# Dynamic convolution and max-out MLP on one core: columns taken in rotated order, and the last weight rows in single loads

## The chip, the cores and the metric

The kernel runs on one core of one Trainium2 chip. Its engines work side by side, each on its own queue of instructions: PE (TensorE, matrix products; PEld are its weight loads), DVE (VectorE, elementwise work), ACT (ScalarE, activations and copies), POOL (GpSimd, here mostly an issuer of DMAs) and SP (SyncE, an issuer of DMAs). 16 DMA engines move data between HBM and the on-chip memory SBUF, whose 128 partitions are the rows of every tile. The metric is the device time of one execution in microseconds (us); a time given for a kernel is the median of several runs.

## The reference

There are 8 sequences of 4160 tokens, 192 features each, and for each token 8 heads with 7 generated weights. Each head mixes a token with the six before it, and the result goes through a max-out MLP:

```python
w = softmax(weight_gen)                       # (8, 4160, 8 heads, 7 taps)
x_pad = concat([zeros(8, 6, 192), x], axis=1) # six zero tokens ahead of every sequence
y[b, s, h, :] = sum(w[b, s, h, k] * x_pad[b, s + k, h, :] for k in range(7))
g = maximum(y @ w1, y @ w2)                   # w1, w2: 192 x 1024
out = g @ w_out                               # 1024 x 192
```

The kernel computes the max-out as relu(y (w2 - w1)) @ w_out + y (w1 @ w_out).

## The kernel before, in words

**Tiling.** The 33280 tokens are laid out with 260 consecutive ones in each of 128 partitions; token number c of each partition is called column c. 16 partitions (RPB) hold one sequence. A token needs the six before it (PAD), so column 0 of a partition needs the last six columns of the partition before, and zeros in every 16th partition, where a sequence starts. These six columns are the halo.

**Batches, pieces, units.** Columns are taken in 17 batches (BATCHES, line 50): 16 of 16 columns, then one of 4. A batch is multiplied and added up in pieces (line 53): of 4 columns in the first two batches, of 8 later, and one of 4 in the last batch. Each piece is one unit: its result y_t is turned around into yt, by PE (sum_transpose) in the first two batches, by a DMA transpose on SP (transpose, line 212) later. A unit of 8 columns gives 8 tiles of hidden products; a unit of 4 gives 4, whose products are 256 wide instead of 512, and twice as many (chunks, line 270).

**A column's way.** load_wg (line 101) brings the generated weights, load_x (line 110) the columns of x as bf16, load_halo (line 123) the six columns ahead of a batch, copied out of the batch before in SBUF. ACT takes exponentials (exp_sum), DVE sums them (red), ACT takes the logarithm (ln), DVE subtracts it (shift), ACT takes exponentials again (weights: en_t). DVE multiplies x by the weights for all seven taps in one instruction (mul, line 173, into m_t) and adds the taps in three (adds, line 188). After the turn, PE makes hidden tiles (hid_tile, line 291, from wd = w2 - w1), ACT takes Relu (relu, line 306, into rd_t), PE makes the outputs (out_first, out_second) from rd_t with wo = w_out and from yt with w10 = w1 @ w_out, ACT copies them out of PSUM (evac, line 377) and SP stores them.

**Order.** The order is written out by hand (a manual schedule). Hidden tiles go in groups (GROUPS), two at a time at the start and three later, and each group has a list of output columns made beside it (OUTS). The steps of the convolution are tied to tile numbers: extra (line 758) says at which tile of batch b the multiplications, additions and transposes of batch b + 1 are issued, and the table due (line 731) when the exponentials are. transpose(u) also issues stores that were held back, and lets POOL wait for the transposed tile (gate) before it issues the next loads of x.

**The start** (lines 520 to 630). SP loads, in this order: the generated weights of batch 0; the halo of batch 0 into xs, in two loads of 15 and 112 partitions, partition 0 being zeroed by DVE; columns 0 to 3; the first halves (512 of 1024 columns) of rows 0 to 127 of w1 and w2 (ws0E, ws1E); the last 64 rows of both (ws0T, ws1T), each in two loads, columns 0 to 511 into partitions 0 to 63 and columns 512 to 1023 into partitions 64 to 127; columns 4 to 7; the second halves of ws0E and ws1E; the generated weights of batch 1. POOL and DVE build a mask msk that is 0 in every 16th partition; DVE and ACT multiply the halo by it (lines 568 and 570) into xb_t. On DVE follow the cast of columns 0 to 3 (line 574), the first multiplication, the differences of the weights' first halves (line 584) and of the last 64 rows (line 589), the cast of columns 4 to 7 (line 620) and the second multiplication. ACT and DVE then copy parts of the differences across the partition halves (lines 586, 587 and 591). PE is kept busy by products that nobody reads (keep_warm, line 612) until the first tiles are there.

**The end.** The last transposes stand in the order of extra; evac stores the last units in smaller parts, and the very last pair of column groups goes out from o_last through ACT's and SP's queues.

Of the kernel before, what the change touches and what calls it, by code (L numbers as in the profile page):

```python
# [23 lines left out]
def kernel(  # L24
# [9 lines left out]
    nc = tc.nc  # L34
# [15 lines left out]
    BATCHES = [(c, min(16, CPP - c)) for c in range(0, CPP, 16)]  # L50
    NB = len(BATCHES)


    def pieces(b):
        n = BATCHES[b][1]
        at, done = [], 0
        for w in (4, 4, 4, 4) if b < 2 else (8, 8) if n == 16 else (n,):
            at.append((done, w))
            done += w
        return at  # L60
# [40 lines left out]
    def load_wg(b, eng):  # L101
        c0, n = BATCHES[b]
        wg_ts[b] = pwg.tile([P, n * WGC], FP32, name="wg_t", tag="wg")
        return eng.dma_start(
            out=wg_ts[b],
            in_=bass.AP(tensor=weight_gen.tensor, offset=c0 * WGC,
                        ap=[[CPP * WGC, P], [1, n * WGC]]),
        )

    def load_x(b, o, n, halo=True):  # L110

        if b not in xb_ts:
            xb_ts[b] = pxb.tile([P, (16 + PAD) * D], BF16, name="xb_t", tag="xb")
        load = nc.gpsimd.dma_start(  # L114
            out=xb_ts[b][:, (PAD + o) * D:(PAD + o + n) * D],
            in_=bass.AP(tensor=x.tensor, offset=(BATCHES[b][0] + o) * D,
                        ap=[[CPP * D, P], [1, n * D]]),
        )
        if b > 0 and o == 0 and halo:
            load_halo(b)  # L120
        return load

    def load_halo(b):

        if b not in xb_ts:
            xb_ts[b] = pxb.tile([P, (16 + PAD) * D], BF16, name="xb_t", tag="xb")
        nc.gpsimd.dma_start(out=xb_ts[b][:, 0:PAD * D],
                            in_=xb_ts[b - 1][:, 16 * D:(16 + PAD) * D])
# [183 lines left out]
    def column(c):  # L312

        b = min(c // 16, NB - 1)
        for u, (ub, o, n) in enumerate(UNITS):
            if ub == b and o <= c - BATCHES[b][0] < o + n:
                k = c - BATCHES[b][0] - o
                return u, k // 2, k % 2
# [58 lines left out]
    def evac(p, n):  # L377
# [3 lines left out]
        if p == NT // 2 - 1:  # L381

            nc.scalar.copy(out=_sub(o_last, 0, [[D, 2], [1, D]]),
                           in_=_sub(tile_, at, [[512, 2], [1, D]]))
            for j, eng in enumerate((nc.scalar, nc.sync)):
                eng.dma_start(
                    out=bass.AP(tensor=out.tensor, offset=(place(p)[0] + 2 * j) * D, ap=[[CPP * D, P], [1, D]]),
                    in_=o_last[:, j * D:(j + 1) * D],
                )
            return  # L390
# [7 lines left out]
        for q in range(p, p + n):  # L398
            u, i, _ = column(2 * q)
            if u == NU - 2 and i % 2:  # L400
# [5 lines left out]
        for eng, c, *ap in stores:  # L406

            def issue(eng=eng, c=c, ap=ap, o=o):
                eng.dma_start(
                    out=bass.AP(tensor=out.tensor, offset=c * D, ap=[[CPP * D, P], *ap]),  # L410
                    in_=_sub(o, c % 24 * D, ap),
                )
# [96 lines left out]
    msk_i = consts.tile([P, 1], I32, name="msk_i")  # L509
    msk = consts.tile([P, 1], FP32, name="msk")  # L510
# [3 lines left out]
    with tc.tile_pool(name="pstage", bufs=1) as pstage:  # L514
# [6 lines left out]
        nc.vector.memset(xs[0:1, 0:PAD * D], 0.0)  # L521
        for p0, p1 in ((1, 16), (16, P)):
            nc.sync.dma_start(
                out=xs[p0:p1, 0:PAD * D],
                in_=bass.AP(tensor=x.tensor, offset=(p0 * CPP - PAD) * D,
                            ap=[[CPP * D, p1 - p0], [1, PAD * D]]),
            )
# [3 lines left out]
        def load_first(o):  # L531
            nc.sync.dma_start(
                out=xs[:, (PAD + o) * D:(PAD + o + 4) * D],
                in_=bass.AP(tensor=x.tensor, offset=o * D, ap=[[CPP * D, P], [1, 4 * D]]),
# [12 lines left out]
        for wi, wsrc in enumerate((moe_w1, moe_w2)):  # L547
            for h in range(2):
                nc.sync.dma_start(
                    out=ws["T", wi][half(h), :],  # L550
                    in_=bass.AP(tensor=wsrc.tensor, offset=P * F + h * HF, ap=[[F, 64], [1, HF]]),
                )
# [4 lines left out]
        nc.gpsimd.iota(msk_i, pattern=[[0, 1]], base=0, channel_multiplier=1)  # L557
        make_identity(nc, ident_f)
        nc.vector.tensor_single_scalar(out=msk_i, in_=msk_i, scalar=RPB - 1, op=ALU.bitwise_and)
        nc.vector.tensor_single_scalar(out=msk_i, in_=msk_i, scalar=1, op=ALU.min)  # L560
        nc.vector.tensor_copy(out=msk, in_=msk_i)
        nc.vector.tensor_copy(out=ident, in_=ident_f)  # L562
        for step in (exp_sum, red, ln, shift):
            for i in range(2):
# [3 lines left out]
        nc.vector.tensor_scalar(out=xb_ts[0][:, 0:HP], in0=xs[:, 0:HP], scalar1=msk[:, 0:1], scalar2=None,  # L568
                                op0=ALU.mult)
        nc.scalar.activation(out=xb_ts[0][:, HP:PAD * D], in_=xs[:, HP:PAD * D], func=AF.Copy,  # L570
                             scale=msk[:, 0:1])
# [160 lines left out]
    for c in range(3, NB):  # L732
        soon = c < 8
        parts_ = [(AT.get(('W', c, 0), 16 * (c - 2) + (8 if soon else 10 if c < NB - 1 else 15)), True, lambda c=c: weights(c, 0))]
        if 8 in dict(pieces(c)):
            parts_.append((AT.get(('W', c, 8), 16 * (c - 2) + (14 if soon else 15)), True, lambda c=c: weights(c, 8)))
        if c > 3:
# [20 lines left out]
    def extra(t):  # L758
# [14 lines left out]
        if s == 8 + later and b + 2 < NB:  # L773
            adds(b + 1, 8, beside=lambda i, of: red(b + 3, i, 2) if b + 3 < NB and i < 2 else None)
        if k == n // 4 - 1 and 7 < u + 1 < NU:
# [56 lines left out]
```

## Time and profile before

| what | value |
|---|---|
| median of 3 runs | 409.88 us (408.94 to 411.68) |
| profiled execution: span, first to last instruction | 408.8 us |
| its time outside the span | not on the page; the median above is 1.1 us over the span |
| PE busy | 399.1 us (98%) |
| DVE busy | 373.4 us (91%) |
| ACT busy | 357.2 us (87%) |
| POOL busy | 75.5 us (18%) |
| granted PE clock, mean | 0.999 |
| moved by DMA | 65.68 MB, mean 161 GB/s |

Times in the profile are us from the first instruction. Busy time is not yet a bound: PE's busy time includes the products that keep it warm. The page gives, for groups of instructions, the busy time, the mean of one and the idle time ahead of them with what ended it; the chain that ended last follows the last instruction back to what released it. DVE's last instruction ends at 379.3 us, PE's last at 405.0; the two last stores are issued at 405.5.

### The profile page before, as it was taken

How to read it: one execution, taken by the hardware profiler on the slowest of the kernel's cores; microseconds unless marked ns; L12 is line 12 of the kernel's file. 1: busy time of each engine (PE TensorE's matmuls, PEld its weight loads, DVE VectorE, ACT ScalarE, POOL GpSimd, SP SyncE). 2: the span in 40 equal slices, each digit the busy share in tenths (PEclk: the TensorE clock that was granted, in tenths of full speed). 3: DMA queues.
4: the chain of work that ended last, by engine and by line, in shares of the span. 5: the costliest groups of instructions: out<-in, count | busy, mean ns of one | idle time of the engine just before them, and what ended most of it. 6: DMA issues, size and time to landing. Idle time of an engine off the chain costs nothing.

```text
span 408.8 us, 16064 instructions
## 1 busy us (share of the span) xinstructions
PE 399.1 (98%) x7386; PEld 317.5 (78%) x7386; DVE 373.4 (91%) x217; ACT 357.2 (87%) x424; POOL 75.5 (18%) x101
## 2 busy tenths in 40 slices
PE   7899999999999999999999999999999999999996
PEld 2688999777777877778777777877787776787796
DVE  5999999999999999999999999999999999999100
ACT  6799999999899998999998999998999888988872
POOL 0311011222221022221111222220121221210000
PEclk9999999999999999999999999999999999999999
DMA  8958477667647854965785397478649638643704
GB/s 240 229 118 217 126 148 164 159 150 182 148 102 198 226 129 98 260 167 85 214 231 117 91 256 186 74 243 168 146 98 250 169 59 223 177 88 108 187 35 161
DMA packets 60784, 65.68 MB, mean 161 GB/s; under 512 B 47631, under 2 KB 49039, under 8 KB 60718
## 3 DMA queue, kind: packets, MB, share of 16 engines
q1 hardware_dynamic: 52334, 40.54, 35.6%
q0 software_dynamic: 8240, 24.04, 29.5%
q8 instruction: 57, 0.93, 0.9%
q10 hardware_dynamic: 144, 0.10, 0.1%
q14 instruction: 9, 0.07, 0.1%
HBM read 35.96 MB, written 25.56 MB: 150 GB/s over the span
## 4 chain that ended last, share of the span: by engine, by line
PE 78%; DVE 7%; ACT 7%; DMA 5%; issue 1%; SPq 1%; DVEq 0%; ACTq 0%
PE op_ps L339 36%; PE hd L299 33%; PE op_ps L351 7%; ACT rd_t L309 4%; DVE m_t L182 4%; DMA ws1T<-in_moe_w_dram 2%; DMA out_dram<-o_t 1%; PE hdp L299 1%; PE yps L248 1%; DVE m_t L204 1%; DVE m_t L198 1%; DMA yt<-y_t 1%; ACT en_t L167 1%; ACT o_t L395 1%; DVE y_t L207 0%
## 5 line engine op out<-in xcount | busy, mean ns | idle before, releaser
L309 ACT ACTIVATE rd_t<-hd 128x1024 bf16<-128x1024 f32 (+1 forms) x206 | 234.4, 1188 | 27.8 <-PE hd L299 26.6
L339 PE MATMUL op_ps<-wo,rd_t 64*128 64x192 bf16 x4160 | 211.4, 243 | 0.4 <-issue 0.3
L339 PEld LDWEIGHTS <-rd_t 64*128 64x128 bf16 x4160 | 181.5, 94 | 16.2 <-issue 0.5
L299 PE MATMUL hd<-yt,wd 64*128 64x512 bf16 (+1 forms) x1584 | 187.8, 360 | 0.9 <-DMA yt<-y_t 0.7
L182 DVE TENSOR_TENSOR m_t<-xb_t,en_t 128x10752 bf16<-128x10752 bf16 (+1 forms) x37 | 187.4, 5070 | 0.2
L299 PEld LDWEIGHTS <-wd 64*128 64x128 bf16 x1776 | 94.8, 94 | 42.4 <-issue 2.0
L224 POOL CAST gate<-yt 128x1 f32<-128x1 bf16 x29 | 41.0, 1415 | 264.6 <-DMA yt<-y_t 264.6
L198 DVE TENSOR_TENSOR m_t<-m_t 128x4608 bf16<-128x4608 bf16 (+1 forms) x31 | 75.5, 2434 | 0.1
L395 ACT COPY o_t<-op_ps 128x384 f32<-128x384 f32 (+1 forms) x99 | 57.1, 588 | 13.4 <-PE op_ps L339 13.4
L351 PE MATMUL op_ps<-w,yt 64*128 64x192 bf16 x780 | 55.9, 243 | 0.2 <-ACT o_t L395 0.2
L351 PEld LDWEIGHTS <-yt 64*128 64x128 bf16 x780 | 38.5, 94 | 16.5 <-issue 1.3
L204 DVE TENSOR_TENSOR m_t<-m_t 128x3072 bf16<-128x3072 bf16 (+1 forms) x29 | 50.0, 1723 | 0.1
L167 ACT ACTIVATE en_t<-wg_t 128x896 bf16<-128x896 f32 (+2 forms) x45 | 35.6, 817 | 0.0
L207 DVE TENSOR_TENSOR y_t<-m_t 128x1536 bf16<-128x1536 bf16 (+1 forms) x29 | 27.3, 941 | 0.5
L114 POOL DMA_DIRECT2D xb_t<-in_x_dram x33 | 17.6, 534 | 29.9 <-ACT rd_t L309 18.9
L156 DVE TENSOR_TENSOR wg_t<-wg_t,sum_t 128x280 f32<-128x280 f32 (+5 forms) x46 | 22.0, 480 | 0.0
L147 DVE TENSOR_REDUCE sum_t<-e_t 128x64 f32<-128x448 f32 (+2 forms) x31 | 19.6, 635 | 2.6 <-ACT e_t L135 2.5
L135 ACT ACTIVATE e_t<-wg_t 128x896 f32<-128x896 f32 (+2 forms) x18 | 16.1, 901 | 2.5 <-DMA wg_t<-in_weight_gen_dram 2.5
L309 ACT ACTIVATE rd_t<-hdp 128x1024 bf16<-128x1024 f32 x16 | 16.2, 1031 | 0.6 <-PE hdp L299 0.4
L615 PE MATMUL warm<-ident 128*128 128x512 bf16 x38 | 11.5, 474 | 2.6 <-DVE ident L562 2.6
L299 PE MATMUL hdp<-yt,wd 64*128 64x256 bf16 x192 | 13.5, 270 | 0.3 <-issue 0.2
L248 PE MATMUL yps<-ident,m_t 64*128 64x64 bf16 x600 | 10.5, 191 | 1.5 <-DVE m_t L182 1.5
(45 smaller groups left out, 65.0 us busy)
## 6 DMA issues: line engine op xcount, KB each, us to landing
out_dram<-o_t SPq DMA_DIRECT2D x27, 768.0 KB, 4.9
xb_t<-in_x_dram POOLq DMA_DIRECT2D x30, 384.0 KB, 5.1
wg_t<-in_weight_gen_dram POOLq DMA_DIRECT2D x14, 448.0 KB, 5.4
xb_t<-xb_t POOLq DMA_DIRECT2D x16, 288.0 KB, 5.2
out_dram<-o_t SPq DMA_DIRECT2D x10, 384.0 KB, 3.3
wg_t<-in_weight_gen_dram SPq DMA_DIRECT2D x2, 448.0 KB, 4.5
xs<-in_x_dram SPq DMA_DIRECT2D x2, 384.0 KB, 6.7
xb_t<-in_x_dram POOLq DMA_DIRECT2D x3, 192.0 KB, 5.0
```

What stands on the lines that cost most here:

```text
L156: nc.vector.tensor_tensor(out=w_t, in0=w_t, in1=_sub(s_ts[b], hs.start, [[1, hs.stop - hs.start], [0, K]]), op=ALU.subtract)
L167: nc.scalar.activation(out=_sub(en_ts[b], (o * WGC + j * N * K) * 2, [[2 * N, K], [2, N], [1, 2]]), in_=_sub(wg_ts[b], (o * H + j * N) * K ...
L182: return nc.vector.tensor_tensor(out=m_out, in0=x_in, in1=_sub(en_ts[b], o * WGC * 2, [[2, K * n * H], [0, G // 2], [1, 2]]), op=ALU.mult,)
L198: nc.vector.tensor_tensor(out=taps(0, 1, 3), in0=taps(0, 1, 3), in1=taps(3, 1, 3), op=ALU.add)
L204: nc.vector.tensor_tensor(out=taps(0, 2, 2), in0=taps(0, 2, 2), in1=taps(1, 5, 2), op=ALU.add)
L207: nc.vector.tensor_tensor(out=_sub(y_ts[b], o * D, [[64, 2], [P, 3 * w // 2], [1, 64]]), in0=taps(0, 1, 1), in1=taps(2, 1, 1), op=ALU.add,)
L224: nc.gpsimd.tensor_copy(out=gate, in_=yt[:, 0:1])
L299: nc.tensor.matmul(hid_out(t, f, j), lhsT=wd_at(j, s, f // 4, f % 4 * P, P), rhs=_sub(yt_ts[u][half(j), :], (s + j) % 3 * P, [[3 * P, w // ...
L309: relu_of[t0] = nc.scalar.activation(out=rd[:, k * 1024:(k + n) * 1024], in_=hd[:, at:at + n * 1024], func=AF.Relu)
L339: return nc.tensor.matmul(op_out(c), lhsT=rd[half(r), k * 1024 + at:k * 1024 + at + P], rhs=wo[half(r), f * D:(f + 1) * D], start=False, s ...
L351: nc.tensor.matmul(op_out(c + j), lhsT=yt_ts[u][half(j), (3 * i + (s + j) % 3) * P:(3 * i + (s + j) % 3 + 1) * P], rhs=w10[half(j), s * D: ...
L395: nc.scalar.copy(out=_sub(o, c % 24 * D, [[D, len(qs)], [h * D, 2], [1, D]]), in_=_sub(tile_, at + (qs[0] - p) * D, [[D, len(qs)], [512, 2 ...
```

## The change

Columns are taken in the order 8 to 259, then 0 to 7. The batches stay 17: 15 of 16 columns, one of 12 and one of 8. dcol turns a place in this order into a column in memory, in every load and store.

The halo of the first batch is then columns 2 to 7 of the partition itself, for all 128 partitions: one load, no zeroed partition, no mask, and the two masking products become copies. The halo of the last batch (columns 0 to 7) is what the first one was: the last six columns of the partition before, loaded by POOL from memory into partitions 1 to 127, then zeros into every 16th partition by a second DMA, from a tile of zeros that POOL fills at the start.

The last batches are multiplied in pieces of 8, 4 (batch 15) and 4, 4 (batch 16), with the issue points that these need. Of the stores, the one in two parts stays with a last-but-one unit of 8 columns, which there is no more.

The last 64 rows of w1 and w2 come in one load each: into all 128 partitions, with the source walked as 2 column halves, 64 rows, 512 columns.

```diff
--- before.py
+++ after.py
@@ -47,14 +47,19 @@
     assert RPB * CPP == S
 
 
-    BATCHES = [(c, min(16, CPP - c)) for c in range(0, CPP, 16)]
+    ROT = 8
+    BATCHES = [(c, min(16, CPP - ROT - c)) for c in range(0, CPP - ROT, 16)] + [(CPP - ROT, ROT)]
     NB = len(BATCHES)
+
+    def dcol(c):
+
+        return (c + ROT) % CPP
 
 
     def pieces(b):
         n = BATCHES[b][1]
         at, done = [], 0
-        for w in (4, 4, 4, 4) if b < 2 else (8, 8) if n == 16 else (n,):
+        for w in (4, 4, 4, 4) if b < 2 else (8, 8) if n == 16 else (8, 4) if n == 12 else (4, 4):
             at.append((done, w))
             done += w
         return at
@@ -103,7 +108,7 @@
         wg_ts[b] = pwg.tile([P, n * WGC], FP32, name="wg_t", tag="wg")
         return eng.dma_start(
             out=wg_ts[b],
-            in_=bass.AP(tensor=weight_gen.tensor, offset=c0 * WGC,
+            in_=bass.AP(tensor=weight_gen.tensor, offset=dcol(c0) * WGC,
                         ap=[[CPP * WGC, P], [1, n * WGC]]),
         )
 
@@ -113,7 +118,7 @@
             xb_ts[b] = pxb.tile([P, (16 + PAD) * D], BF16, name="xb_t", tag="xb")
         load = nc.gpsimd.dma_start(
             out=xb_ts[b][:, (PAD + o) * D:(PAD + o + n) * D],
-            in_=bass.AP(tensor=x.tensor, offset=(BATCHES[b][0] + o) * D,
+            in_=bass.AP(tensor=x.tensor, offset=dcol(BATCHES[b][0] + o) * D,
                         ap=[[CPP * D, P], [1, n * D]]),
         )
         if b > 0 and o == 0 and halo:
@@ -124,8 +129,15 @@
 
         if b not in xb_ts:
             xb_ts[b] = pxb.tile([P, (16 + PAD) * D], BF16, name="xb_t", tag="xb")
-        nc.gpsimd.dma_start(out=xb_ts[b][:, 0:PAD * D],
-                            in_=xb_ts[b - 1][:, 16 * D:(16 + PAD) * D])
+        if b < NB - 1:
+            nc.gpsimd.dma_start(out=xb_ts[b][:, 0:PAD * D],
+                                in_=xb_ts[b - 1][:, 16 * D:(16 + PAD) * D])
+            return
+        nc.gpsimd.dma_start(
+            out=xb_ts[b][1:P, 0:PAD * D],
+            in_=bass.AP(tensor=x.tensor, offset=(CPP - PAD) * D, ap=[[CPP * D, P - 1], [1, PAD * D]]),
+        )
+        nc.gpsimd.dma_start(out=xb_ts[b][0:P:RPB, 0:PAD * D], in_=zeros[0:P:RPB, :])
 
 
     def exp_sum(b, i=0, of=1):
@@ -311,10 +323,9 @@
 
     def column(c):
 
-        b = min(c // 16, NB - 1)
-        for u, (ub, o, n) in enumerate(UNITS):
-            if ub == b and o <= c - BATCHES[b][0] < o + n:
-                k = c - BATCHES[b][0] - o
+        for u, (b, o, n) in enumerate(UNITS):
+            k = c - BATCHES[b][0] - o
+            if 0 <= k < n:
                 return u, k // 2, k % 2
 
     def place(p):
@@ -384,7 +395,7 @@
                            in_=_sub(tile_, at, [[512, 2], [1, D]]))
             for j, eng in enumerate((nc.scalar, nc.sync)):
                 eng.dma_start(
-                    out=bass.AP(tensor=out.tensor, offset=(place(p)[0] + 2 * j) * D, ap=[[CPP * D, P], [1, D]]),
+                    out=bass.AP(tensor=out.tensor, offset=dcol(place(p)[0] + 2 * j) * D, ap=[[CPP * D, P], [1, D]]),
                     in_=o_last[:, j * D:(j + 1) * D],
                 )
             return
@@ -397,7 +408,7 @@
         stores = []
         for q in range(p, p + n):
             u, i, _ = column(2 * q)
-            if u == NU - 2 and i % 2:
+            if u == NU - 2 and UNITS[u][2] == 8 and i % 2:
                 stores.append((nc.sync, place(q)[0] - 1, [4 * D, 2], [1, 2 * D]))
             elif u < NU - 1 and i == UNITS[u][2] // 2 - 1:
                 stores.append((nc.sync, place(q)[0] - i, [1, 2 * (i + 1) * D]))
@@ -407,7 +418,7 @@
 
             def issue(eng=eng, c=c, ap=ap, o=o):
                 eng.dma_start(
-                    out=bass.AP(tensor=out.tensor, offset=c * D, ap=[[CPP * D, P], *ap]),
+                    out=bass.AP(tensor=out.tensor, offset=dcol(c) * D, ap=[[CPP * D, P], *ap]),
                     in_=_sub(o, c % 24 * D, ap),
                 )
 
@@ -506,8 +517,7 @@
     wo = consts.tile([P, FCH * D], BF16, name="wo")
     w10 = consts.tile([P, 3 * D], BF16, name="w10")
     ident = consts.tile([P, P], BF16, name="ident")
-    msk_i = consts.tile([P, 1], I32, name="msk_i")
-    msk = consts.tile([P, 1], FP32, name="msk")
+    zeros = consts.tile([P, PAD * D], BF16, name="zeros")
     gate = consts.tile([P, 1], FP32, name="gate")
     o_last = consts.tile([P, 2 * D], FP32, name="o_last")
 
@@ -518,20 +528,17 @@
               for kind, w in (("E", F), ("T", HF)) for wi in range(2)}
 
         load_wg(0, nc.sync)
-        nc.vector.memset(xs[0:1, 0:PAD * D], 0.0)
-        for p0, p1 in ((1, 16), (16, P)):
-            nc.sync.dma_start(
-                out=xs[p0:p1, 0:PAD * D],
-                in_=bass.AP(tensor=x.tensor, offset=(p0 * CPP - PAD) * D,
-                            ap=[[CPP * D, p1 - p0], [1, PAD * D]]),
-            )
+        nc.sync.dma_start(
+            out=xs[:, 0:PAD * D],
+            in_=bass.AP(tensor=x.tensor, offset=(ROT - PAD) * D, ap=[[CPP * D, P], [1, PAD * D]]),
+        )
 
         nc.scalar.preload_act_table_set("natural_log_exp_and_others")
 
         def load_first(o):
             nc.sync.dma_start(
                 out=xs[:, (PAD + o) * D:(PAD + o + 4) * D],
-                in_=bass.AP(tensor=x.tensor, offset=o * D, ap=[[CPP * D, P], [1, 4 * D]]),
+                in_=bass.AP(tensor=x.tensor, offset=dcol(o) * D, ap=[[CPP * D, P], [1, 4 * D]]),
             )
 
         load_first(0)
@@ -545,30 +552,24 @@
 
         load_w(0)
         for wi, wsrc in enumerate((moe_w1, moe_w2)):
-            for h in range(2):
-                nc.sync.dma_start(
-                    out=ws["T", wi][half(h), :],
-                    in_=bass.AP(tensor=wsrc.tensor, offset=P * F + h * HF, ap=[[F, 64], [1, HF]]),
-                )
+            nc.sync.dma_start(
+                out=ws["T", wi],
+                in_=bass.AP(tensor=wsrc.tensor, offset=P * F, ap=[[HF, 2], [F, 64], [1, HF]]),
+            )
         load_first(4)
         load_w(1)
         load_wg(1, nc.sync)
 
-        nc.gpsimd.iota(msk_i, pattern=[[0, 1]], base=0, channel_multiplier=1)
+        nc.gpsimd.memset(zeros, 0.0)
         make_identity(nc, ident_f)
-        nc.vector.tensor_single_scalar(out=msk_i, in_=msk_i, scalar=RPB - 1, op=ALU.bitwise_and)
-        nc.vector.tensor_single_scalar(out=msk_i, in_=msk_i, scalar=1, op=ALU.min)
-        nc.vector.tensor_copy(out=msk, in_=msk_i)
         nc.vector.tensor_copy(out=ident, in_=ident_f)
         for step in (exp_sum, red, ln, shift):
             for i in range(2):
                 step(0, i, 2)
         xb_ts[0] = pxb.tile([P, (16 + PAD) * D], BF16, name="xb_t", tag="xb")
         HP = PAD * D // 4
-        nc.vector.tensor_scalar(out=xb_ts[0][:, 0:HP], in0=xs[:, 0:HP], scalar1=msk[:, 0:1], scalar2=None,
-                                op0=ALU.mult)
-        nc.scalar.activation(out=xb_ts[0][:, HP:PAD * D], in_=xs[:, HP:PAD * D], func=AF.Copy,
-                             scale=msk[:, 0:1])
+        nc.vector.tensor_copy(out=xb_ts[0][:, 0:HP], in_=xs[:, 0:HP])
+        nc.scalar.copy(out=xb_ts[0][:, HP:PAD * D], in_=xs[:, HP:PAD * D])
         for o in (0, 4, 8, 12):
             weights(0, o)
         nc.vector.tensor_copy(out=xb_ts[0][:, PAD * D:(PAD + 4) * D],
@@ -734,6 +735,8 @@
         parts_ = [(AT.get(('W', c, 0), 16 * (c - 2) + (8 if soon else 10 if c < NB - 1 else 15)), True, lambda c=c: weights(c, 0))]
         if 8 in dict(pieces(c)):
             parts_.append((AT.get(('W', c, 8), 16 * (c - 2) + (14 if soon else 15)), True, lambda c=c: weights(c, 8)))
+        if 4 in dict(pieces(c)):
+            parts_.append((16 * (c - 2) + 18, True, lambda c=c: weights(c, 4)))
         if c > 3:
             ln_at = -2 if c == 4 else 0 if c < 8 else 2 if c < 11 else 4
             parts_.append((AT.get(('l', c, 0), 16 * (c - 2) + ln_at), False, lambda c=c: ln(c)))
@@ -772,6 +775,9 @@
             mul(b + 1, 8)
         if s == 8 + later and b + 2 < NB:
             adds(b + 1, 8, beside=lambda i, of: red(b + 3, i, 2) if b + 3 < NB and i < 2 else None)
+        if s == 8 and b + 2 == NB:
+            mul(b + 1, 4)
+            adds(b + 1, 4)
         if k == n // 4 - 1 and 7 < u + 1 < NU:
             transpose(u + 1)
 
```

## The prediction

> **What bounds the kernel now.** I read the page first, then the table by stretches of time, the chain of work that ended last, the waits, and the start and end engine by engine.
>
> ```profile
> PE 399.1 (98%) x7386; PEld 317.5 (78%) x7386; DVE 373.4 (91%) x217; ACT 357.2 (87%) x424; POOL 75.5 (18%) x101
> 61.00:345.00 284.00, 283.04 (x4926) 221.95 (x4921) 283.59 (x157) 258.12 (x291) 60.26 (x72) 1.00 0.68 162
> PE hd L299 <- DMA yt<-y_t: 0.7, 1, 0.7
> ```
>
> The second line is the stretch from 61 to 345 us: its length, then busy time of PE, PEld, DVE, ACT, POOL. PE (283.04) and DVE (283.59) are both full, so the body is bound twice: DVE makes the columns, PE uses them, at one pace. The third line is PE's only wait on the way, 0.7 us at 345 us, for a transposed tile from DVE. So a delay at the start that hits both engines is not won back: PE has 0.7 us in hand and DVE nothing. After 345 us the chain is PE alone, to 405.0.
>
> The start is where the change works:
>
> ```profile
> 5.42 7.69 DMA ws1T<-in_moe_w_dram
> 13.11 0.04 DVEq L589
> 13.15 0.04 issue
> 13.19 0.69 DVE wd L589
> 13.88 0.01 issue
> 13.89 0.97 DVE xb_t L620
> ...
> 14.96 2.97 DVE m_t L182
> 17.93 0.05 issue
> 17.98 1.42 PE yps L248 x84
> ```
>
> This chain (start, length, what) says: the last 64 rows of w1 and w2 (ws0T, ws1T) land at 13.1; the subtraction at L589 waits for them, and behind it on DVE stand the cast L620 and the second multiplication L182, for which PE waits. DVE had been idle 0.51 us ahead of L589, and 0.83 us ahead of the first cast (8.45, for xs). From there it has no gap.
>
> How fast those loads run, and on how many DMA engines, decides the case. First the stretches of the start (the last two numbers are the busy share of 16 DMA engines and GB/s), then the DMA queue of SP from 0 to 17 us:
>
> ```profile
> 4.50:6.80 2.30, 2.30 (x7) 0.75 (x5) 1.68 (x4) 1.56 (x4) 0.00 (x0) 1.00 0.97 279
> 6.80:8.50 1.70, 1.70 (x5) 0.61 (x4) 0.87 (x3) 1.68 (x4) 0.00 (x0) 1.00 1.04 373
> 8.50:10.50 2.00, 2.00 (x10) 0.93 (x9) 1.90 (x2) 2.00 (x7) 0.00 (x0) 1.00 1.07 231
> q1 hardware_dynamic: 1630, 3.86, 76.1%
> ```
>
> The engines are full in all three. Loads of 128 partitions (6.8 to 8.5) reach 373 GB/s, that is 23.3 GB/s for each engine. Where the four half loads of 64 partitions run (8.5 to 10.5) it is 231; around the halo loads of 15 and 112 partitions 279.
>
> The 1630 packets can be counted out. The 14 loads have 128 + 15 + 112 + 128 + 4x128 + 4x64 + 128 + 128 = 1407 rows; 223 packets remain, which is 13x16 + 15. So each load closes with one packet for each engine that it used: 16 where its outer count is 128, 112 or 64, and 15 where it is 15. The number of engines follows the outermost count of the transfer.
>
> **The change, part by part.**
>
> *Weight rows.* Four half loads become two of 256 KB. Each source has an outermost count of 2 (the column half), then 64 rows of 2 KB; its target has 128 partitions. By the count above, a transfer cut along 2 goes to 2 engines. I take this value; the other end is 16. On two engines, each carries 128 KB of ws0T and 128 KB of ws1T: 262 KB at 23.3 GB/s is 11.25 us. They start where they start now, at about 8.5, since the loads ahead of them on the queue are the same bytes: done at 19.75. Into that stretch fall POOL's loads for columns 8 to 15 and for w_out (now issued 12.4 to 14.5): (2x393 + 786) KB / 16 = 98 KB for each engine, 4.2 us if all of it goes ahead, so 24.0 at the latest. I take the middle, 21.9, against 13.19 now: L589 starts **8.7 us later**. The cast L620 needs the second piece of xs, now queued behind ws1T: 24.6 KB an engine, 1.05 us, of which 0.69 lie beside L589: **0.35 more**. Behind L589 wait the whole of DVE, ACT's copies L591 (and so the first tile on PE, whose weights they are) and POOL's loads that follow the first Relu; nothing useful is left to do meanwhile, so all of it reaches the end.
>
> The Trainium skill, DMA: Bandwidth & Descriptors, section Why a DMA increments its semaphore by 16 and not by 1, states it as a rule: the number of engines is the largest up to 16 that divides the slowest count, other than 1, of both sides. By that rule these loads run on 2 engines and the sum is the one above; the trace agrees as far as the 15 closing packets of the 15-partition load go, and it shows no load whose two sides differ.
>
> *First halo.* One load of 128 partitions for two (15 and 112), same bytes (590 KB). At 373 instead of 279 GB/s it takes some 0.6 us less; between 0 and 0.6 for all that follows. This would bring the first multiplication forward by as much (xs waits 0.83; its weights are ready at 8.35), but L589 then waits all the longer: nothing of it is left in the forecast. Memset, mask steps and iota go from DVE and POOL (1.02, 0.08, 0.15, 0.15 and 0.12 us), all in DVE's idle time before 5.12: nothing. The mask's products L568 and L570 become copies of the same size: nothing.
>
> *Zeros.* A memset of 128x1152 now precedes the identity on POOL. The 128x128 f32 one takes 0.20; nine times the elements, 4.5 times the bytes: 0.9 to 1.8 us. DVE's identity copy moves from 2.4 to 4.1 at most, still before 5.12; PE's 30 warming products start later, covered by the wait for the weights. Nothing; without that wait up to 1 us.
>
> *SP's queue.* Three issues fewer (0.32 to 0.64 each). SP's last four loads of the start wait for earlier landings (6.75, 8.44, 9.73, 10.96) and go earlier now, into queues that are full: nothing gained, and they pass the two busy engines only after ws1T. The second halves of w1 and w2 need 1.4 us more there and are wanted 4.65 us after L589: covered.
>
> *The last batches,* 16 + 4 columns, become 12 + 8, in pieces of 8, 4, 4, 4. On DVE a piece of 8 takes 11.05 us (362.32 to 373.37) and one of 4 takes 5.93 (to 379.30): three of 4 for one of 8 and one of 4 cost 0.8 us more. The last transposed tile lands at 383.1 and PE wants it at 391.2; with 0.8, the wait for its weights on ACT (1.1) and SP's store between the two transposes (383.8, then 1.4 to issue and 3.7 to land), it lands at 389: covered by 2 us. ACT has one exponential of 0.61 more and one 0.46 shorter; its gaps here are 0.3 to 0.6 each: nothing. On PE four pairs of tiles go in 24 products of 256 instead of 12 of 512, 1.36 against 1.34 us in the chain: **0.1**. The stores keep number and place.
>
> *Last halo.* From DRAM in 127 rows, then zeros to 8 partitions once it has landed. Issued at 357.5 (5.3 us to land, like POOL's loads), the second 0.55 and 4.1: 367.5, and the multiplication can start at 369.3, when its weights are there. Behind it on POOL are only the gate copies of 366.4 on, for which nobody waits. Nothing.
>
> **Sum:** 8.7 + 0.35 + 0.1 = 9.1 us on the span of 408.8, so 417.9. The page gives no time outside the span; the median of the runs, 409.88, is 1.1 above it, and I carry that along: **419.0 us**. Its own range: 415 (start at 7.9, after a faster halo, at 25 GB/s an engine, no POOL traffic: 18.4) to 423 (24.0, and 1 us for a cold start of PE and the spread of the runs).
>
> **The rivals.**
>
> 1. *All 16 engines serve the new weight loads.* For it: the 128 target partitions, and no row with unequal sides. Then they run at 373 instead of 231 GB/s, land over a microsecond earlier, L589's 0.51 us of waiting goes, and with the halo another 0 to 0.6: 0.5 to 1.1 us faster, **409.1**. It decides as soon as ws1T lands before 13. Next in line is then DVE itself.
>
> 2. *The last halo runs on one engine.* 127 has no divisor up to 16 but 1, and this load, too, is told apart by its count. 127 rows of 4.6 KB at 23.3 GB/s: 25 us, landing near 383, the zeros near 388, two steps of DVE (5.93) and a transpose (5.0) later 399, and PE wants that tile at 385.7: 13 us more. It decides from a landing later than about 369. Alone **422**, with the slow weight loads 432. Against it: POOL's descriptors are another queue, and every row of it here has 128 partitions. The Trainium skill (same page and section) gives one engine for 127 partitions, but names some loads issued from GpSimd that put 127 on all 16; no row here shows either.
>
> **Chances.** The forecast 0.63: one odd count in the trace was followed to the packet. Rival 1 0.20. Rival 2 0.04 alone, 0.10 with the slow weights. The rest 0.03. From 408.5 to 423 lies about 0.8. Under 1% (4.1 us) is what I call no change here: faster 0.02, same 0.20, slower 0.78.
>
> **What would show it.** Right: SP's two weight loads take over 13 us to land where they now take 8; DVE idle 6 to 11 us before the subtraction of ws1T; DMA at about 50 GB/s and two engines' share in that stretch; the same shift of everything after; the last 40 us alike. The queue's packets at the start then count 128 + 128 + ... rows and two closings for each weight load. Wrong: ws1T landing before 13, or a wait on the last halo at 370 to 390.

## The result

| | before | after |
|---|---|---|
| median of 4 runs | 410.46 us (408.94 to 411.68) | 422.72 us (421.78 to 424.37) |
| ratio | | 1.0305 [1.0271 to 1.034], slower |
| span of the profiled execution | 408.8 us | 420.0 us (its own time 421.78) |

The forecast was 419.0 (408.5 to 423). The sign and the cause came out as predicted. The loss is larger than the 9.1 us of the forecast: 11.2 in the spans, 12.3 in the medians. The result lies 0.3 us under the top of the range, and a later section shows that this was partly luck. (One more run of the kernel before stands in this table than in the one above.)

### The profile page after: what moved, and what is told of

Its sections match the earlier page's. It is cut to its first block, busy times and chain, and to the rows that moved or that the text cites. A ratio compares the mean times of both kernels' runs of the same rounds, so it can differ in the third digit from the quotient of the medians.

```text
span 420.0 us, 16160 instructions
## 1 busy us (share of the span) xinstructions
PE 400.7 (95%) x7434; PEld 321.5 (77%) x7434; DVE 372.4 (89%) x217; ACT 357.1 (85%) x425; POOL 78.3 (19%) x103
## 4 chain that ended last, share of the span: by engine, by line
PE 86%; DMA 6%; ACT 6%; SPq 1%; issue 1%; DVE 0%; ACTq 0%; DVEq 0%
PE op_ps L350 39%; PE hd L311 36%; PE op_ps L362 7%; DMA ws1T<-in_moe_w_dram 5%; ACT rd_t L321 3%; PE hdp L311 2%; PE yps L260 1%; DMA yt<-y_t 1%; ACT en_t L179 1%; ACT o_t L406 0%; ACT yt L267 0%; ACT w1t L676 0%; SPq L548 0%; DVE wd L590 0%; SPq L555 0%
## 5 line engine op out<-in xcount | busy, mean ns | idle before, releaser
L311 PEld LDWEIGHTS <-wd 64*128 64x128 bf16 x1824 | 97.5, 95 | 52.6 <-issue 13.2
L236 POOL CAST gate<-yt 128x1 f32<-128x1 bf16 x30 | 42.0, 1400 | 264.0 <-DMA yt<-y_t 264.0
L311 PE MATMUL hdp<-yt,wd 64*128 64x256 bf16 x192 | 14.6, 293 | 11.1 <-ACT yt L267 10.8
L168 DVE TENSOR_TENSOR wg_t<-wg_t,sum_t 128x280 f32<-128x280 f32 (+6 forms) x46 | 22.1, 481 | 0.3 <-ACT sum_t L163 0.3
L159 DVE TENSOR_REDUCE sum_t<-e_t 128x64 f32<-128x448 f32 (+3 forms) x31 | 19.6, 636 | 2.1 <-ACT e_t L147 2.1
L616 PE MATMUL warm<-ident 128*128 128x512 bf16 x38 | 10.9, 455 | 2.6 <-DVE ident L565 2.6
L260 PEld LDWEIGHTS <-m_t 64*128 64x128 bf16 x600 | 10.7, 99 | 1.7 <-issue 0.8
```

The lines of the kernel that those rows point to most:

```text
L168: nc.vector.tensor_tensor(out=w_t, in0=w_t, in1=_sub(s_ts[b], hs.start, [[1, hs.stop - hs.start], [0, K]]), op=ALU.subtract)
L236: nc.gpsimd.tensor_copy(out=gate, in_=yt[:, 0:1])
L311: nc.tensor.matmul(hid_out(t, f, j), lhsT=wd_at(j, s, f // 4, f % 4 * P, P), rhs=_sub(yt_ts[u][half(j), :], (s + j) % 3 * P, [[3 * P, w // ...
```

## The profile after

First the page's busy times:

```profile
PE 400.7 (95%) x7434; PEld 321.5 (77%) x7434; DVE 372.4 (89%) x217; ACT 357.1 (85%) x425; POOL 78.3 (19%) x103
```

Then the stretch from 61 to 345 us (length, busy PE, PEld, DVE, ACT, POOL, granted clock, DMA share, GB/s):

```profile
61.00:345.00 284.00, 283.76 (x4990) 224.71 (x4987) 283.56 (x157) 258.74 (x292) 62.27 (x73) 1.00 0.67 163
```

And two of PE's waits (total, times, longest):

```profile
PE hdp L311 <- ACT yt L267: 10.8, 1, 10.8
PE hd L311 <- DMA yt<-y_t: 0.8, 1, 0.8
```

Nothing is busy for noticeably longer than before. PE has a wait of 10.8 us ahead of its first tile, for ACT's copies, and the body is as full on PE and DVE as it was, so nothing of that wait is won back. The chain of waits names what ACT waited for (start, length, what; pieces under 0.05 us left out):

```profile
3.86 19.47 DMA ws1T<-in_moe_w_dram
...
23.42 0.70 DVE wd L590
...
24.15 0.62 ACT wd L592
...
24.79 0.81 ACT yt L267
...
25.64 2.75 PE hdp L311 x24
```

The single load of the last w2 rows, issued at 3.86, landed at 23.33; the subtraction that needs it (L589 before, L590 now) started at 23.42 instead of 13.19. DVE's own instructions (start, length, operation, and the idle time ahead with what ended it), first two of the kernel before:

```profile
9.12 2.96 DVE L182 TENSOR_TENSOR m_t<-xb_t,en_t 128x5376 bf16<-128x5376 bf16 x1
13.19 0.69 DVE L589 TENSOR_TENSOR wd<-ws1T,ws0T 128x512 bf16<-128x512 f32 x1 [0.51 <-DMA ws1T<-in_moe_w_dram]
```

Then those of the changed kernel:

```profile
7.65 2.96 DVE L194 TENSOR_TENSOR m_t<-xb_t,en_t 128x5376 bf16<-128x5376 bf16 x1
10.52 0.68 DVE L585 TENSOR_TENSOR wd<-ws1E,ws0E 128x512 bf16<-128x512 f32 x1
23.42 0.69 DVE L590 TENSOR_TENSOR wd<-ws1T,ws0T 128x512 bf16<-128x512 f32 x1 [12.22 <-DMA ws1T<-in_moe_w_dram]
24.65 0.56 DVE L621 CAST xb_t<-xs 128x768 bf16<-128x768 f32 x1 [0.53 <-DMA xs<-in_x_dram]
```

The first multiplication, at 7.65, is 1.47 earlier than before (9.12): the halo in one load helps there (an experiment below takes it back), and all of it is spent in the 12.22 us of idle time that follow. What the loads looked like meanwhile (stretches, columns as above):

```profile
6.80:8.50 1.70, 1.70 (x8) 0.74 (x7) 1.60 (x4) 1.70 (x7) 0.00 (x0) 1.00 0.47 175
8.50:10.50 2.00, 2.00 (x11) 0.93 (x10) 2.00 (x1) 1.27 (x4) 0.00 (x0) 1.00 0.13 49
```

SP's DMA queue from 0 to 30 us (packets, MB, share of 16 engines):

```profile
q1 hardware_dynamic: 1556, 3.87, 38.2%
```

A DMA share of 0.13 is 2 engines of 16, and 49 GB/s is 24.5 for each; before, the same stretch had 1.07 and 231 GB/s. The 1556 packets are 1408 rows and 148 closings: nine loads with 16 and the two weight loads with 2 each. In stretches of 0.2 us the share falls to 0.12 at 7.6, so the two engines work alone from about there.

That 14 engines had nothing to do, although more loads stood ready behind, shows in SP's issues (start, length):

```profile
3.86 0.58 SPq L555 DMA_DIRECT2D ws1T<-in_moe_w_dram  x1
4.48 5.92 SPq L539 DMA_DIRECT2D xs<-in_x_dram  x1
10.46 0.42 SPq L548 DMA_DIRECT2D ws0E<-in_moe_w_dram  x1
```

The issue behind ws1T, the second piece of x, held SP for 5.92 us; the second halves of w1 and w2 and the next generated weights could only be handed over after 10.4, and POOL's loads, which follow the first multiplication, came at the same time. A single issue of over 1 us at the start stands only in the runs whose weight loads use two engines (5.92, 2.01 and 1.86 here; 3.67 and 2.93 in t_only below). That a queue of the two busy engines was full is the likely reason; the profile doesn't show it.

From there the shift is passed on: second multiplication 14.96 to 25.32 (+10.4), last addition for the tile that PE waits for in the body 339.18 to 349.83 (+10.7), end of that wait 345.13 to 356.07 (+10.9), PE's last output products 402.82 to 414.10 (+11.3).

The last halo, the other load with an odd count, is here (POOL's issues, then both loads with KB and us from issue to landing, then the multiplication that needs them):

```profile
374.10 0.57 POOL L140 DMA_DIRECT2D xb_t<-zeros  x1 [5.21 <-DMA xb_t<-in_x_dram]
```

```profile
xb_t<-in_x_dram POOLq DMA_DIRECT2D x1, 285.8 KB, 5.5
xb_t<-zeros POOLq DMA_DIRECT2D x1, 18.0 KB, 3.9
```

```profile
380.30 2.96 DVE L194 TENSOR_TENSOR m_t<-xb_t,en_t 128x5376 bf16<-128x5376 bf16 x1 [0.93 <-ACT en_t L179]
```

The 127 rows landed in 5.5 us, the zeros at 378.0; DVE had 0.93 us to wait at 380.3, and for ACT. This load costs nothing.

## The experiments

The theory: the two single weight loads run on two engines, because their source is walked with an outermost count of 2, and everything lost at the end is the wait for them. Rivals: the slow clock that PE has after its long pause; POOL's loads ahead on the same engines; a loss through the rotated order itself; and, for the cause of the two engines, that one load into 128 partitions from 64 rows is slow for another reason than the count. Times are medians, each with its ratio to the kernel before on the same chip (410.64 to 410.78 in the three sets).

### Each half of the change alone

**rot_only** is the changed kernel with the four half loads back:

```diff
-            nc.sync.dma_start(out=ws["T", wi],
-                in_=bass.AP(..., offset=P * F, ap=[[HF, 2], [F, 64], [1, HF]]))
+            for h in range(2):
+                nc.sync.dma_start(out=ws["T", wi][half(h), :],
+                    in_=bass.AP(..., offset=P * F + h * HF, ap=[[F, 64], [1, HF]]))
```

**t_only** is the kernel before with only the opposite edit.

> The changed kernel with the last 64 weight rows loaded as before, in four half loads of 64 partitions. Theory (the two single weight loads run on 2 of 16 engines and are the whole loss): DVE starts its first multiplication at 7.65 us as in the changed kernel (before: 9.12), the subtraction of the last rows at about 12 instead of 13.19; 1.2 us gained at the start, 0.3 us given back at the end (PE's narrower tiles and one more exponential on ACT), so 0.9 us faster than before: ratio 0.996 to 0.999. Rival (the rotated order costs, too: its last batches, its last halo or the zeros): slower than before by 1 us or more, ratio above 1.0025.

> The kernel before with nothing changed but the last 64 weight rows, in one load each for w1 and w2, source walked as 2 halves, 64 rows, 512 columns. Theory: these loads start on two engines at about 8.5 us, carry 262 KB on each at 24.6 GB/s (10.7 us) and share the engines with POOL's loads; the subtraction starts at 23 to 24.5 instead of 13.19, and the time is 10.5 to 12 us over before: ratio 1.026 to 1.029. Rival (the single loads cost little by themselves, it is their mix with the rotated order): ratio under 1.01.

Measured: rot_only 409.87 us, 0.9976 [0.9952 to 0.9999]; t_only 423.07 us, 1.0268 [1.0231 to 1.0306]. The whole loss is in the weight loads. SP's queue in t_only has 1570 packets: 1407 rows, and 163 closings, which are nine loads with 16, the halo of 15 partitions with 15 and the two weight loads with 2 each. DVE in t_only (start, length, idle ahead):

```profile
22.76 0.69 DVE L588 TENSOR_TENSOR wd<-ws1T,ws0T 128x512 bf16<-128x512 f32 x1 [10.65 <-DMA ws1T<-in_moe_w_dram]
```

The same wait, with nothing rotated. The profiled execution of rot_only showed a pause of 2.0 us on PE at 23 to 25 us that waited for nothing the profile shows, and its span, 410.6, was the longest of all its executions. So the same kernel was run once more:

> rot_only once more, the same kernel, for its profile and as the measure of single16. In its first profile PE had 2.0 us of issue ahead of the third turn of tiles by PE, then a granted clock of 0.76 from 24 to 31 us, and that execution was the slowest of its twelve (412.37). If that stretch is chance, this profile has a shorter one, its span is 407.5 to 408.5 and the median 408.9 to 410; if it belongs to the earlier start, it is there again.

Measured: 409.18 us, 0.9961 [0.9939 to 0.9983], span 406.9, without that pause. DVE's subtraction starts at 11.34 with no wait, the second multiplication at 12.59 (14.96 before), PE's last products at 400.87 (402.82). This version is faster than the kernel before by 0.9 us in its first measurement and by 1.5 in its second, with intervals that reach from almost nothing to 2.5.

### Is it the count or the single load?

**single16** is the changed kernel; the same single load of 256 KB into the same 128 partitions, with the source walked as 128 rows:

```diff
-                in_=bass.AP(..., offset=P * F, ap=[[HF, 2], [F, 64], [1, HF]]),
+                in_=bass.AP(..., offset=P * F, ap=[[HF, P], [1, HF]]),
```

> The changed kernel, each single weight load with the same 256 KB, the same bytes of memory and the same 128 target partitions, but walked in the order of memory: 128 rows of 2 KB, outermost count 128 instead of 2. The rows so land in other partitions than the product needs: what is computed from the last 64 weight rows is wrong, the time is that of the same work. Theory (the outermost count of 2 is the whole loss): 16 engines, the last rows land by 11, no wait ahead of their subtraction, which starts at 11.0 to 11.6; time as rot_only or up to 0.5 us under it, ratio to the kernel before 0.995 to 0.999. Rival (one load per weight is slow because of its size or its 128 partitions): ratio above 1.01.

Measured: 408.80 us, 0.9952 [0.9932 to 0.9972]. Stretch of the loads, and the subtraction:

```profile
8.50:10.50 2.00, 2.00 (x11) 0.79 (x9) 2.00 (x1) 1.43 (x5) 0.00 (x0) 1.00 1.05 408
```

```profile
11.28 0.68 DVE L590 TENSOR_TENSOR wd<-ws1T,ws0T 128x512 bf16<-128x512 f32 x1
```

SP's queue in single16 from 0 to 24 us:

```profile
q1 hardware_dynamic: 1584, 3.87, 43.8%
```

The wait is gone. The 1584 packets are 1408 rows and 176 closings, 16 for each of the 11 loads. The load of ws1T landed 6.2 us after its issue instead of 19.47. The share in this stretch went from 0.13 to 1.05 and the rate from 49 to 408 GB/s; the loads behind have their part in that, since SP was not held. Bytes, partitions and number of loads are the same. So neither the single load nor its target is slow; only the walk of the source differs. The walk also makes the rows contiguous, so a dose was wanted that keeps the four half loads and changes the count alone.

**split4** was the first attempt, on the kernel before:

```diff
-                    in_=bass.AP(..., ap=[[F, 64], [1, HF]]),
+                    in_=bass.AP(..., ap=[[16 * F, 4], [F, 16], [1, HF]]),
```

> The kernel before; the four half loads keep their bytes, their 64 target partitions and their place, but the 64 source rows are written as 4 groups of 16, outermost count 4 instead of 64. Theory (the number of engines follows the outermost count that the instruction carries): 4 engines carry 131 KB each at 24.6 GB/s, 5.3 us from about 8.5, more with POOL's share; the last rows land at 14 to 17 instead of 13.1, 1 to 4 us slower, and each such load closes with 4 packets instead of 16 (48 packets fewer at the start). Rival (what counts is the number of partitions or of bytes, not how the rows are written): time and packets as before.

Measured: 410.49 us, 0.9993 [0.9971 to 1.0015], and the queue has 1630 packets as before, where four closings for each of these loads would give 1582. The 4 and the 16 have a common step, so they are one count of 64 in another spelling; the packets fit 16 engines, so they were evidently joined again before the engines were chosen. It told nothing of the dose. **strided4** and its control **strided16** take steps that can't be joined:

```diff
-                    in_=bass.AP(..., ap=[[F, 64], [1, HF]]),
+                    in_=bass.AP(..., ap=[[F, 4], [4 * F, 16], [1, HF]]),     # strided4
+                    in_=bass.AP(..., ap=[[F, 16], [16 * F, 4], [1, HF]]),    # strided16
```

> The kernel before; its four half loads take the 64 rows as 4 groups with a step that can't be joined to one count (rows a, a+4, a+8, ... for a = 0 to 3): outermost count 4, same bytes and partitions. The rows land in another order, so what is computed from them is wrong. Theory: 4 engines with 131 KB each at 24.6 GB/s, 5.3 us from about 8.5, plus what POOL's loads take there: the subtraction starts at 14.2 to 16.5 instead of 13.19, 1 to 3 us slower, ratio 1.0025 to 1.008; 1582 packets of SP's queue at the start instead of 1630 (4 closings for 16, four times). Rival (a step in the rows is slow by itself, or the count plays no part): as strided16.

> The control of strided4: the same, with 16 groups of 4 rows (rows a, a+16, a+32, a+48), outermost count 16; what is computed from the last 64 rows is wrong here, too. Theory: 16 engines, 1630 packets, the subtraction at 12.7 to 13.3, ratio 0.998 to 1.002.

Measured: strided4 415.55 us, 1.0119 [1.0083 to 1.0156]; strided16 410.19 us, 0.9988 [0.9963 to 1.0012]. SP's queue in strided4 from 0 to 24 us, and its subtraction:

```profile
q1 hardware_dynamic: 1582, 3.86, 56.7%
```

```profile
16.95 0.69 DVE L589 TENSOR_TENSOR wd<-ws1T,ws0T 128x512 bf16<-128x512 f32 x1 [4.34 <-DMA ws1T<-in_moe_w_dram]
```

1582 is exactly what four closings for each of the four loads give; strided16 has 1630. The wait is 4.34 us where two engines give 12.22, and none with 16. The kind of effect is as forecast; the price, 4.9 us against the 1 to 3 expected, is larger. Against its control strided4 is 5.4 us slower, and its subtraction starts 4.95 later (16.95 and 12.00): here, too, the wait is the loss.

### How long does it take on two engines, and what stands ahead?

**after_again** is the changed kernel once more, as the mate of the next two. **pool_later** holds POOL's first three loads (columns 8 to 15, w_out) until the subtraction of the last rows instead of the first multiplication:

```diff
-        behind(first_mul, load_x(0, 8, 4))
+        behind(t_sub, load_x(0, 8, 4))
```

> The changed kernel once more, as the measure for the two runs beside it: ratio 1.028 to 1.034, as in its first measurement.

> The changed kernel with POOL's first three loads (columns 8 to 15 of the rotated order and w_out) held until the subtraction of the last weight rows, so that the two busy engines have nothing else to carry. Theory (POOL's 98 KB on each of them stand ahead of the last weight rows): ws1T lands at 18.5 to 19.5 instead of 23.3, and the subtraction starts 4 us earlier; part of it is lost again because columns 8 to 15 then land about 5 us after it, near the time at which DVE wants them: 2 to 4 us gained, ratio to the changed kernel 0.990 to 0.995. Rival (the two engines are slow by themselves, 19.5 us of flight without POOL's loads too): ws1T lands at 22 or later and nothing is gained.

Measured: after_again 421.96 us, 1.0272 [1.0247 to 1.0297], subtraction at 23.64; pool_later 419.32 us, 1.0213 [1.0185 to 1.024]:

```profile
20.22 0.69 DVE L590 TENSOR_TENSOR wd<-ws1T,ws0T 128x512 bf16<-128x512 f32 x1 [8.98 <-DMA ws1T<-in_moe_w_dram]
```

POOL's loads were worth 3.4 us of the landing against after_again (2.8 to 3.4 against the three traces in which they go early: after, after_again and, below, warm), and 2.6 in the time. They are no second cause: rot_only has them as well, and DVE doesn't wait. Without them two engines still end at 20.2, later than forecast. At the 50 GB/s of the stretch from 8 to 10 us, 524 KB take 10.5 us from 7.6: 18.1. The stretches of pool_later show what may fill the remaining 2 us:

```profile
8.00:10.00 2.00, 2.00 (x10) 0.88 (x9) 2.00 (x1) 1.80 (x6) 0.00 (x0) 1.00 0.13 51
12.00:14.00 2.00, 2.00 (x89) 1.59 (x89) 0.00 (x0) 0.52 (x1) 0.00 (x0) 1.00 1.03 260
18.00:20.00 2.00, 0.00 (x0) 0.00 (x0) 0.00 (x0) 0.00 (x0) 0.00 (x0) 0.64 0.13 49
```

From 10.5 to 16 the other 14 engines carry SP's later loads. Nearly all 16 are then busy, in the middle of it at 260 GB/s, 16 each, and if our two also run at 16 for those 5.5 us they lose some 48 KB, about 2 us. That is an estimate; the trace has no rate for a single engine.

### Is PE's slow clock a part of the loss?

In the changed kernel PE has nothing to do from 14.8 to 25.64. **warm** gives it products that nobody reads through the pause:

```diff
         sum_transpose(0)
-        keep_warm(8)
+        keep_warm(52)
         mul(0, 4)
```

> The changed kernel with 52 instead of 8 of the products that nobody reads while PE waits for the weights, so that PE is busy until about 24 us. In the changed kernel PE's granted clock is 0.50 from about 17 to 31 us, and PE falls from 10.2 to 11.65 us behind the kernel before. Theory (PE has about 0.7 us in hand against DVE by 345 us, and DVE lost only 0.3 us to the slow clock): the clock stays at 1.0 and 0.3 to 0.6 us are gained, ratio to the changed kernel 0.9985 to 0.9993. Rival (all that PE lost in the slow stretch reaches the end): 1.3 to 1.5 us gained, ratio 0.9965 to 0.997. Second rival: the clock falls all the same.

Measured: 421.96 us, 1.0271 [1.0248 to 1.0294], the same median as after_again. Both kernels' stretches (the third number from the right is the granted clock), first after_again, then warm:

```profile
18.00:24.00 6.00, 0.00 (x0) 0.00 (x0) 0.36 (x1) 0.00 (x0) 0.00 (x0) 0.50 0.64 152
24.00:31.00 7.00, 5.14 (x112) 4.22 (x113) 6.27 (x9) 5.24 (x7) 1.16 (x2) 0.50 0.23 33
```

```profile
18.00:24.00 6.00, 6.00 (x29) 2.72 (x28) 0.69 (x1) 0.22 (x1) 0.00 (x0) 1.00 0.61 135
24.00:31.00 7.00, 5.21 (x144) 4.04 (x141) 6.54 (x8) 6.34 (x9) 1.09 (x2) 1.00 0.39 56
```

The clock stays full in warm and PE's first tiles take 1.49 instead of 2.74 us, yet no gain is measured at the end. DVE, which has no reserve in the body, gets its last rows at nearly the same time in both (23.06 in warm, 23.64 in after_again). Neither the gain of 0.3 to 0.6 us that the theory gave nor the 1.3 to 1.5 of the rival shows; a small one can't be excluded, since each interval reaches about 1 us to either side.

### What the first halo is worth

**rot_halo2** is rot_only with the first halo in two loads again, of partitions 0 to 15 and 16 to 127:

```diff
-        nc.sync.dma_start(out=xs[:, 0:PAD * D], in_=bass.AP(..., ap=[[CPP * D, P], [1, PAD * D]]))
+        for p0, p1 in ((0, 16), (16, P)):
+            nc.sync.dma_start(out=xs[p0:p1, 0:PAD * D],
+                in_=bass.AP(..., ap=[[CPP * D, p1 - p0], [1, PAD * D]]))
```

> As rot_only, but the first halo in two loads, of partitions 0 to 15 and 16 to 127, as near as it comes to the two of before. Theory (one load of 128 partitions runs at the full rate, the load of 112 partitions does not, so that xs lands later): first multiplection of DVE at 8.3 to 9.1 instead of 7.65, the time 0.3 to 1.2 us over rot_only. Rival (the first multiplication is early because the mask and the zeroed partition are gone from DVE and ACT): first multiplication at 7.65 to 8, time as rot_only.

Measured: 409.97 us, 0.998 [0.9961 to 0.9998]. The first multiplication starts at 8.98, in the two traces of rot_only at 7.84 and 7.86:

```profile
8.98 2.96 DVE L194 TENSOR_TENSOR m_t<-xb_t,en_t 128x5376 bf16<-128x5376 bf16 x1
7.86 2.96 DVE L194 TENSOR_TENSOR m_t<-xb_t,en_t 128x5376 bf16<-128x5376 bf16 x1
```

So the single load brings it 1.1 us forward. The other traces agree: with two halo loads the multiplication starts between 8.52 and 9.21 (six traces), with one between 7.65 and 7.90 (seven), and rot_halo2 has no mask either. In the time the two can't be told apart: 409.97 against 409.87 and 409.18.

## Why the prediction was right, and where it was short

**Two engines: right.** The packet count that the forecast named (rows and two closings for each weight load), 49 GB/s and the two engines' share are all there. DVE's idle time is 12.22 where 6 to 11 was forecast, also because the first multiplication came 1.47 earlier. t_only and single16 show from both sides that it is the cause, strided4 and strided16 that the outermost count sets it. The Trainium skill's rule (DMA: Bandwidth & Descriptors, Why a DMA increments its semaphore by 16 and not by 1: the largest count up to 16 that divides the slowest counts of both sides) agrees with all that was counted here: 2, 4, 15 and 16. Rival 1, all 16 engines for the new loads, is refuted for this walk of the source; single16 shows what it would have given: 1.8 us less than the kernel before (1.1 to 2.8 by its interval), where I had put 0.5 to 1.1.

**The landing: the mis-sized term.** Forecast 21.9, measured 23.4. Two parts of the sum were too small. I took half of POOL's 4.2 us as ahead of the last rows; pool_later shows 2.8 to 3.4, that is 0.7 to 1.3 more than the 2.1 in the sum. And 23.3 GB/s for each of the two engines throughout gave 19.75; without POOL's loads it was 20.2, although the two started 0.9 earlier than I had them (7.6 against 8.5). Their rate was slightly above 23.3 while they were alone, and by the estimate above about 16 beside the others.

**The cast behind it: nearly right.** DVE waits 0.53 us for the second piece of x, a little over the 0.35 of the sum, but the cast itself takes 0.56 instead of 0.96. The second multiplication is 10.36 later, against 10.23 for the subtraction, so 0.13 is added.

**No delay is won back: right.** PE and DVE are both full from 61 to 345, and the shift goes through. It even grows, from 10.36 at the second multiplication to 10.94 at the end of PE's wait at 345. Of these 0.6 us, which the sum had at nothing, 0.3 lie in the flight of the transposed tile (4.80, now 5.09); the cause of the rest is open.

**The end: right in kind.** From the end of PE's wait for the transposed tile (345.13, now 356.07) to its last products it took 57.69 us before and 58.03 after, 57.74 in rot_only_b: 0.05 to 0.34 more, forecast 0.1. The last transposed tile let POOL's gate go at 401.4, PE used it at 402.6: 1.2 us of cover instead of 2.

**The first halo: right for this kernel, too small by itself.** I gave it 0 to 0.6 us and hid it. It was hidden; but the single load alone brings the first multiplication 1.1 us forward, and with the weights in half loads DVE's second multiplication comes 2.4 earlier (14.96 to 12.59), of which 0.9 to 1.5 us show in the two medians of rot_only. How much of that is the halo's own is not shown, since the times of rot_only and rot_halo2 can't be told apart.

**SP's queue: wrong in detail.** "Go earlier now, into queues that are full: nothing gained" overlooked that the issue itself can take 5.92 us. Three of the four loads went later than before, not earlier (handed over from 10.46 to 12.97, before from 8.44 to 10.96), and the second stretch of full engines then fell into the time when the two were still at work.

**The last halo, rival 2: refuted.** 127 rows from POOL took 5.5 us, not 25. The 285.8 KB that landed are 53 GB/s, twice what one engine carried in the weight loads. The Trainium skill's exception for some loads issued from GpSimd (same page and section), which the rival had against it, agrees as far as the time goes; the engines of this load were not counted. **Zeros: right,** nothing: the identity's copy on DVE stands at 2.33, before 2.37. **The cold start of PE: right** to leave out of the sum; the clock did fall, and warm gained nothing that can be measured.

**The time outside the span: a term too small.** I carried 1.1 us along, the median of the runs less the span of one. The later runs come with the span of each execution: the time outside is 1.73 to 3.07 us, in the middle 1.8, and 1.78 in the profiled execution of the changed kernel.

**The whole account.** From 419.0 to 422.72 are 3.7 us. The landing gives 1.5 of them (the subtraction starts 10.23 later, not 8.7), the cast takes back 0.2, the body adds 0.6 and the end 0.2: the 2.1 by which the spans differ from the forecast. The time outside adds 0.7, and 0.9 is spread, since the profiled execution was the fastest of the four. That 422.72 still lies under 423 is partly luck. That end of the range was made of a landing at 24.0, which came near (23.4), and of 1 us for PE's cold start and the spread; it was filled by the body and the time outside as well, for which nothing had been set aside. after_again's median is 421.96, 11.2 above its mate.

## What to carry to other kernels

Fewer DMAs are not faster DMAs: before two loads are joined into one, read the outermost count of the new one's source and target, since a 2 there put 256 KB on 2 engines (49 GB/s) and the same 256 KB in 128 rows ran on 16 (landed after 6.2 us instead of 19.5). Count the closing packets of the queue against its rows: that tells how many engines the loads of a profile used, and from one odd count, like the 15 here, what a new load may do; only a run of the change settled it. And where two engines both fill the body, as here, a delay of the first operand is paid in full at the end, however much idle time stands around it.

## What the runs showed of the hardware that was not expected

- An issue on SP can take 5.92 us instead of some 0.4, while 2 of 16 DMA engines are busy (7.6 to 10.4 us). Every load behind it waits, even for engines that stand idle. That a full queue holds it is likely and not shown.
- Counts that have a common step are evidently one count, however they are written: 4 times 16 rows in split4 kept 1630 packets, the interleaved 4 times 16 in strided4 had 1582.
- PE's granted clock fell to 0.50 at 17.7 us, 2.9 into the pause of 10.8, and was full again only at 31.3, 5.7 after PE's work began again. Keeping it full gained nothing that could be measured. That DVE set the pace meanwhile is the likely reason; no run tested it by itself.
- In stretches of 0.2 us, the time at 0.50 lasted 13.65 us in the changed kernel and in after_again, 10.24 in t_only, 6.82 in pool_later, and 3.41 in strided4 and rot_only. All six are multiples of 3.41, as if the clock were decided at fixed intervals; that is a reading of six traces, which no run tested.
- PE once paused for 2.0 us at 23 to 25 us with nothing to wait for in the profile (rot_only), and not when the same kernel ran again. The clock was at 0.50 from 25.2 to 28.6 after it.
